# Order edges that hold each weight block's first-layer matmuls behind attention issued two blocks earlier

## The chip, the cores and the metric

The kernel runs on one core of one Trainium2 chip. The core has a matrix engine (TensorE, PE in the profile, with its weight loads shown apart as PEld), a vector engine (DVE), a scalar engine (ACT), GpSimd (POOL), and SyncE (SP), which here only starts transfers. Each engine works through its own list of instructions in order and waits on semaphores for the others. The metric is the device time of one execution in microseconds; less is better.

## The reference, cut to what matters

Everything is float32. Three stages follow each other, and each takes all of the one before:

```python
# 1. attention, batch 4, 8 heads, 512 local and 32 global positions, head size 64
s_g   = scale * q_g @ concat(k_g, k_l).T            # global queries see everything
out_g = softmax(s_g) @ concat(v_g, v_l)
s_ll  = where(abs(i - j) <= 32, scale * q_l @ k_l.T, -1e9)
a_l   = softmax(concat(scale * q_l @ k_g.T, s_ll))  # local ones a window and the globals
out_l = a_l @ concat(v_g, v_l)
x = concat(out_g, out_l) as (4, 576, 512)
# 2. first network, 512 -> 2048 -> 512, with a norm ahead and the input added back
xn = (x - mean) / sqrt(var + 1e-6) * g_ln
x  = x + relu(xn @ w_ch1) @ w_ch2
# 3. second network, 512 -> 1024 -> 512, gated by a 3-wide convolution over the sequence
h   = relu(x @ w_in)
out = (h * sigmoid(conv3(h))) @ w_out
```

## The kernel before, in words

**Attention** works on items. A local item is one batch, one tile of 128 queries and one pair of heads (64 of them, four to a tile); a global item is one batch and one pair of heads (16, spread among the local ones by `GAT`). An item takes these steps: its rows are loaded (`raw`), queries and keys are split into a rounded part and a remainder (`qs` on DVE and POOL, `kh` on ACT, `kl` on POOL), PE forms scores (`ps`, L273 and L274; a global item in two halves, L371 and L372), DVE takes them out of PSUM with mask and maximum (L277, L375), ACT does the exponentials (L286, L380), PE transposes (`pt` L299, `ptg` L393), ACT copies the result out (`ptsb`), and PE multiplies by the values (`po` L314 to L320, `pog` L402). Four items complete a tile; it is normed (`xn`, L443), transposed on PE (`ptx`, L455), and split by ACT and DVE (L106, L113) into `xe` or `xo`, which the first network reads. From item 23 on, all scores use one PSUM bank (`ps_a`, tag "s"), one unit of scores after the other. The first 16 items are a prologue of their own.

**The first network** works on chunks of tiles: one of three tiles, then seven of two (`CHUNKS`). Even chunks read `xe`, odd ones `xo`. For each chunk it goes through 16 weight blocks. A weight block is `hidden1` (12 first-layer matmuls of 256 columns, L669, into `ph`), a relu on ACT and its remainder on DVE (`hh` and `hl`, L678 and L679), and one block later `out1` (for each tile two matmuls on `hh` and one on `hl`, L692 to L697, into `yps`). I count blocks through: block 18 is the third block of chunk 1. In chunk 0 the third tile's `yps` occupies the bank "s".

**What sets the order.** The program is traced once and then put in order by a list scheduler: on each engine it issues, of what is ready by its own estimate of times, what has the best priority. Attention steps are traced from `tick` (L719), which is called some times in each block and hands `attend` (L518) a target that grows with the chunk (`PACE`), so that chunk c+1 is due a quarter chunk before chunk c ends. Within `attend` the steps get a priority 300 places ahead (`ahead(B_ATT)`). Nothing but readiness and priority ties the first network's matmuls to attention, other than the data: the first block of a chunk needs that chunk's `xe` or `xo`. In the last chunk (chunk 7) no attention is left, and the second network follows it.

Of the kernel before, what the change touches and what calls it, by code (L numbers as in the profile page):

```python
# [17 lines left out]
P = 128  # L18
# [4 lines left out]
NF, NF2, NDC = FF // P, F2 // P, DM // P  # L23
# [25 lines left out]
PACE = (0.25, 0), (0.88, 1), (1.8, 2), (2.75, 3)  # L49
CLEAD = 3.25  # L50
YLAG = 1
HB2 = 2

LATE = 7
# [7 lines left out]
def f32(ap):  # L62
    return ap.bitcast(F32)
# [3 lines left out]
def tile_kernel(ctx: ExitStack, tc: tile.TileContext, a_w, a_e, a_m, g_qk, g_v, w12, g_ln, w_io, conv_w, out):  # L67
    nc = tc.nc
    PE, DVE, ACT, POOL, SP = nc.tensor, nc.vector, nc.scalar, nc.gpsimd, nc.sync
# [14 lines left out]
    @contextmanager  # L84
    def ahead(n):
        p = tc.cur_priority
        tc.cur_priority = p - n
        yield
        tc.cur_priority = max(p, tc.cur_priority + n)

    def traced():
        return nc.cur_bb.bb.instructions
# [338 lines left out]
    chunks, at = [], 0  # L431
# [83 lines left out]
        add_step(i)  # L515
    pos = [0]

    def attend(upto):  # L518
        while pos[0] < min(upto, len(micro)):
            with ahead(B_ATT):  # L520
                micro[pos[0]]()
            pos[0] += 1

# [24 lines left out]
    def load_next(upto):  # L550
        while nload[0] < min(upto, NF if wpos[0] >= wdone[NF - 2] else NF - 1):
            load_w(nload[0], nload[0], w12[nload[0]])
            nload[0] += 1

    def convert(upto):
        while wpos[0] < min(upto, len(wq)):
            wq[wpos[0]]()
            wpos[0] += 1
# [18 lines left out]
    for i in range(first):  # L577
        slot, at = slots[i // PER], i % PER * RWH
# [7 lines left out]
    for k in range(1, len(slots)):  # L586
        n = min(PER, first - k * PER) * RWH
# [56 lines left out]
    def store_y(key, x):  # L644
        if key == "g":
            for b in range(B):
                SP.dma_start(yscr[b * S:b * S + SG, :], x[b * SG:(b + 1) * SG])
        else:
            b, t = key
            r = b * S + SG + t * P  # L650
            SP.dma_start(yscr[r:r + P, :], x)

    def first_network(items, tick, after_y, hpool, y_banks):

        hts, yps = {}, {}

        def edge(k, d):
            return not 0 <= k + d < len(items) or items[k + d][0] != items[k][0]

        def hidden1(k):  # L660
            ci, f = items[k]
            n = len(chunks[ci]) * P
            xth, xtl = xts[ci]
            convert(wdone[f])
            wh, wl = wt[f]
            ph = ps_h.tile([P, DM], F32, tag="h", name="ph")
            terms = [(w, x, d) for w, x in ((wh, xth), (wl, xth), (wh, xtl)) for d in range(NDC)]
            for m, (w, x, d) in enumerate(terms):
                PE.matmul(ph[:, :n], w[:, d * P:(d + 1) * P], x[:, d], start=m == 0, stop=m == 3 * NDC - 1)  # L669
                if m == 5:  # L670
                    tick(k)
            hh = hpool.tile([P, n], F32R, tag="hh", name="hh", bufs=HB2)
            if n > 2 * P:
                hl = early[:, k % 2 * n:][:, :n]
            else:
                hl = hpool.tile([P, n], F32R, tag="hl", name="hl", bufs=HB2)
            with ahead(B_RELU):
                ACT.activation(hh, ph[:, :n], AF.Relu)  # L678
                DVE.scalar_tensor_tensor(hl, ph[:, :n], 0.0, f32(hh), op0=ALU.max, op1=ALU.subtract)  # L679
            hts[k] = hh, hl  # L680
            tick(k)

        def out1(k):
            ci, f = items[k]
            hh, hl = hts.pop(k)
            wh, wl = wt[f]
            for i, key in enumerate(chunks[ci]):
                if edge(k, -1):
                    pool, tag = y_banks[i]
                    yps[i] = pool.tile([P, DM], F32, tag=tag, name="yps")  # L690
                tk = slice(i * P, (i + 1) * P)
                PE.matmul(yps[i], hh[:, tk], wh[:, DM:], start=edge(k, -1), stop=False)  # L692
                PE.matmul(yps[i], hh[:, tk], wl[:, DM:], start=False, stop=False)  # L693

            for i, key in enumerate(chunks[ci]):
                tk = slice(i * P, (i + 1) * P)
                PE.matmul(yps[i], hl[:, tk], wh[:, DM:], start=False, stop=edge(k, 1))  # L697
                if edge(k, 1):
                    x = xtiles[key].x
                    DVE.scalar_tensor_tensor(x, yps[i], xtiles[key].rstd, x, op0=ALU.mult, op1=ALU.add)  # L700
                    if f == NF - 1:
                        store_y(key, x)
                tick(k)
            after_y(k)

        for k in range(len(items) + YLAG):
            if k < len(items):
                hidden1(k)
            if k >= YLAG:
                out1(k - YLAG)  # L710

    last = len(chunks) - 1
    items = [(ci, f) for ci in range(last) for f in range(NF)]
    ends_at = [0] + [max(need[k] for k in chunks[ci + 1]) for ci in range(last)]
# [4 lines left out]
    def tick(k):  # L719
        ci = k // NF  # L720
        ticks[ci] += 1
        beats = 2 + CHUNKS[ci]
        at = ci + ticks[ci] / (beats * NF)
        for (t0, c), (t1, _) in zip(pace, pace[1:]):
            if t0 < at:
                attend(ends_at[c] + int((ends_at[c + 1] - ends_at[c]) * min((at - t0) / (t1 - t0), 1)))
        if ci == 0:
            load_next(LD3 + k)
            x = CLEAD + ticks[0] / beats
            done = [0] + [wdone[f] for f in range(NF)]  # L730
            f = int(x)
            convert(done[f] + int((done[f + 1] - done[f]) * (x - f)) if f < NF else done[NF])

    first_network(items, tick, lambda k: None, mpool,
                  [(ps_y, "y0"), (ps_y, "y1"), (ps_a, "s")])
    attend(len(micro))
    pa.close()

# [252 lines left out]
```

## Time and profile before

| | |
|---|---|
| runs, us | 765.64, 761.85, 766.15 (median 765.64) |
| profiled execution, us | 761.55 |
| its span, us | 759.7 |
| instructions in the span | 13043 |
| PE busy | 737.9 us, 97% |
| PEld / DVE / ACT / POOL busy | 87% / 60% / 48% / 31% |
| mean granted TensorE clock | 0.993 |

All other numbers are from the one profiled execution. Its own time is 1.85 us more than its span (761.55 against 759.7). Chunk 0 runs up to about 126 us, chunks 1 to 6 with attention beside them up to about 445 us in all, and after that PE has no attention left.

### The profile page before, as it was taken

The numbers are of one execution on the slowest core, as the hardware profiler recorded it, in microseconds if no ns is written. First come the engines' busy times: TensorE is split into PE (matmuls) and PEld (weight loads), VectorE is DVE, ScalarE is ACT, GpSimd is POOL, SyncE is SP. The second block draws the span as 40 slices with busy tenths as digits, with TensorE's granted clock in tenths as the row PEclk, the third lists the DMA queues.
The fourth block names the chain that finished last, engine by engine and source line by source line (L and its number), as shares of the span: only waits on it lengthen the run. The fifth ranks groups of instructions, "written<-read, shape, count | busy, mean of one in ns | idle before, by whom it ended". The sixth has DMA issues, their size and how long they took to land.

```text
span 759.7 us, 13043 instructions
## 1 busy us (share of the span) xinstructions
PE 737.9 (97%) x4841; PEld 664.7 (87%) x4841; DVE 457.7 (60%) x995; ACT 366.9 (48%) x871; POOL 235.4 (31%) x280
## 2 busy tenths in 40 slices
PE   9889999999999899989999999999999999999997
PEld 5778798998899799989998999998899998898996
DVE  4879974458564757576565743124966664555552
ACT  6768742456455455554544642114743353543431
POOL 1024330335343434454433530001324332332321
PEclk9999999999999899999999999999999999999999
DMA  9992231232433322243323310009520020200101
GB/s 371 425 415 82 76 111 38 70 94 84 125 88 99 110 79 85 84 130 100 87 75 102 84 35 28 0 19 354 206 83 1 1 86 16 81 4 1 57 1 69
DMA packets 30527, 77.08 MB, mean 101 GB/s; under 512 B 3712, under 2 KB 9856, under 8 KB 27392
## 3 DMA queue, kind: packets, MB, share of 16 engines
q1 hardware_dynamic: 29936, 75.42, 29.3%
q8 instruction: 38, 0.62, 0.3%
q10 hardware_dynamic: 528, 0.84, 0.3%
q14 instruction: 25, 0.20, 0.1%
HBM read 67.33 MB, written 8.91 MB: 100 GB/s over the span
## 4 chain that ended last, share of the span: by engine, by line
PE 55%; ACT 0%; DVE 0%; ACTq 0%; issue 0%
PE ph L669 12%; PE ph L829 4%; PE ph L831 4%; PE ph L830 4%; PE yps L697 4%; PE po L848 4%; PE yps L692 4%; PE yps L693 4%; PE po L849 4%; PE po L850 4%; PE pty L762 1%; PE pt L299 1%; PE po L320 1%; PE ps L274 1%; PE ps L273 1%; PE pog L402 0%
## 5 line engine op out<-in xcount | busy, mean ns | idle before, releaser
L669 PE MATMUL ph<-xe,w 128*128 128x256 f32 (+1 forms) x768 | 120.2, 300 | 4.7 <-ACT xe L106 3.5
L669 PEld LDWEIGHTS ph<-xe,w 128*128 128x128 f32 x768 | 110.7, 191 | 11.0 <-ACT xe L106 4.0
L669 PE MATMUL ph<-xo,w 128*128 128x256 f32 x768 | 111.1, 286 | 2.2 <-ACT xo L106 2.2
L113 POOL TENSOR_TENSOR kl<-raw,kh 128x384 fp32r<-128x384 f32 (+2 forms) x64 | 77.0, 1203 | 113.6 <-ACT kh L106 104.0
L692 PE MATMUL yps<-w,hh 128*128 128x512 f32 x272 | 110.1, 405 | 0.8 <-DVE x L330 0.4
L669 PEld LDWEIGHTS ph<-xo,w 128*128 128x128 f32 x768 | 103.1, 191 | 6.9 <-ACT xo L106 2.4
L693 PE MATMUL yps<-w,hh 128*128 128x512 f32 x272 | 107.9, 397 | 0.0
L678 ACT ACTIVATE hh<-ph 128x256 fp32r<-128x256 f32 (+1 forms) x128 | 50.2, 393 | 97.2 <-PE ph L669 89.7
L113 POOL TENSOR_TENSOR gl<-c,gh 128x544 fp32r<-128x544 f32 x32 | 44.2, 1380 | 135.6 <-ACT gh L106 135.6
L679 DVE SCALAR_TENSOR_TENSOR hl<-ph,hh 128x256 fp32r<-128x256 f32 x112 | 46.8, 419 | 64.6 <-ACT hh L678 63.6
L829 PE MATMUL ph<-yth,w 128*128 128x272 f32 x256 | 74.9, 293 | 0.0
L831 PE MATMUL ph<-yth,w 128*128 128x272 f32 x256 | 73.9, 289 | 0.0
L830 PE MATMUL ph<-ytl,w 128*128 128x272 f32 x256 | 73.8, 288 | 0.0
L697 PE MATMUL yps<-w,hl 128*128 128x512 f32 x224 | 72.7, 400 | 0.3 <-DVE hl L679 0.3
L286 ACT ACTIVATE sm<-sm,nm 128x192 f32<-128x192 f32 (+1 forms) x128 | 58.5, 459 | 16.5 <-DVE nm L277 16.1
L277 DVE CUSTOM_DVE_ANT_0 sm<-ps,mask 128x192 f32<-128x192 f32 (+1 forms) x128 | 42.3, 368 | 39.3 <-PE ps L274 28.7
L244 POOL TENSOR_TENSOR qs<-raw,qs 64x256 fp32r<-64x256 f32 x48 | 39.6, 824 | 68.6 <-ACT kh L106 22.7
L106 ACT ACTIVATE kh<-raw 128x384 fp32r<-128x384 f32 (+2 forms) x64 | 36.8, 577 | 49.7 <-issue 27.5
L692 PEld LDWEIGHTS yps<-w,hh 128*128 128x128 f32 x272 | 51.2, 188 | 7.7 <-ACT hh L678 1.0
L693 PEld LDWEIGHTS yps<-w,hh 128*128 128x128 f32 x272 | 51.3, 188 | 5.9
L834 DVE TENSOR_SCALAR c<-hs,cw 128x544 f32<-128x544 f32 x32 | 26.1, 816 | 49.9 <-ACT hs L832 48.0
L837 ACT ACTIVATE c<-c 128x544 f32<-128x544 f32 x32 | 21.1, 658 | 71.5 <-DVE c L836 68.9
(143 smaller groups left out, 1565.5 us busy)
## 6 DMA issues: line engine op xcount, KB each, us to landing
wraw<-w SPq DMA_DIRECT2D x16, 1024.0 KB, 17.1
raw<-a_m SPq DMA_DIRECT2D x24, 352.0 KB, 3.0
wraw<-w_io SPq DMA_DIRECT2D x8, 1024.0 KB, 6.6
raw<-a_e SPq DMA_DIRECT2D x25, 320.0 KB, 2.9
raw<-g_qk SPq DMA_DIRECT2D x16, 304.0 KB, 2.8
rawg<-g_v SPq DMA_DIRECT2D x16, 280.0 KB, 2.9
yr<-yscr SPq DMA_DIRECT2D x16, 256.0 KB, 3.4
yscr<-x SPq DMA_DIRECT2D x15, 256.0 KB, 2.0
```

The source lines that it names most:

```text
L113: e_lo.tensor_tensor(lo, src, f32(hi), op=ALU.subtract)
L277: DVE.tensor_tensor_reduce(out=s, in0=ps[j][:, :w], in1=mask[:, self.m0:self.m0 + w], scale=-0.125, scalar=BIG, op0=ALU.add, op1=ALU.min, ...
L286: ACT.activation(s, s, AF.Exp, bias=self.nm[:, j:j + 1], scale=-1.0, accum_out=xt.sums[:, h:h + 1])
L669: PE.matmul(ph[:, :n], w[:, d * P:(d + 1) * P], x[:, d], start=m == 0, stop=m == 3 * NDC - 1)
L678: ACT.activation(hh, ph[:, :n], AF.Relu)
L679: DVE.scalar_tensor_tensor(hl, ph[:, :n], 0.0, f32(hh), op0=ALU.max, op1=ALU.subtract)
L692: PE.matmul(yps[i], hh[:, tk], wh[:, DM:], start=edge(k, -1), stop=False)
L693: PE.matmul(yps[i], hh[:, tk], wl[:, DM:], start=False, stop=False)
L697: PE.matmul(yps[i], hl[:, tk], wh[:, DM:], start=False, stop=edge(k, 1))
L829: PE.matmul(ph, wh[:, w], yth[:, d, tk], start=d == 0, stop=False)
L830: PE.matmul(ph, wh[:, w], ytl[:, d, tk], start=False, stop=False)
L831: PE.matmul(ph, wl[:, w], yth[:, d, tk], start=False, stop=d == NDC - 1)
```

## The change

`attend` now notes for each of its PE instructions the block `k` in whose ticks it was traced. `hidden1(k)` wraps each of its twelve matmuls in `held(k)`: it looks up the last PE instruction of attention that was traced in block `k - 2` or earlier and adds an order edge behind it. The edge has no semaphore. It only tells the scheduler that on PE this matmul may not stand ahead of that instruction. No operation is added, removed or changed in size.

```diff
+HOLD = 2
-    def attend(upto):
+    issued = []
+
+    def attend(upto, k=0):
+        at = len(traced())
         while pos[0] < min(upto, len(micro)):
             with ahead(B_ATT):
                 micro[pos[0]]()
             pos[0] += 1
+        issued.extend((k, ins) for ins in traced()[at:] if ins.engine == mybir.EngineType.PE)
+
+    def held(k):
+
+        own = [ins for at, ins in issued if at <= k - HOLD]
+        return tc.issue_after(own[-1]) if own else nullcontext()
...
-                PE.matmul(ph[:, :n], w[:, d * P:(d + 1) * P], x[:, d], start=m == 0, stop=m == 3 * NDC - 1)
+                with held(k):
+                    PE.matmul(ph[:, :n], w[:, d * P:(d + 1) * P], x[:, d], start=m == 0, stop=m == 3 * NDC - 1)
...
-                attend(ends_at[c] + int((ends_at[c + 1] - ends_at[c]) * min((at - t0) / (t1 - t0), 1)))
+                attend(ends_at[c] + int((ends_at[c + 1] - ends_at[c]) * min((at - t0) / (t1 - t0), 1)), k)
```

Up to the first-layer matmuls of block 18 PE's list is the same as before. From there to the end of chunk 6 it differs; behind that it is the same again. Three places follow. Line numbers of the change are 11 higher for first-layer matmuls (L680) and `out1` (L703 to L708), and 1 higher for attention.

**Place 1**, PE's list at the start of chunk 1, behind the score unit `ps_1309`. `ph_1447`, `ph_1522`, `ph_1580` are the first-layer outputs of blocks 18, 19, 20; `ps_1367` and `ps_1395` are the halves of the next (global) item, `pt_1356` the transposes of the item of `ps_1309`. Before:

```order
L697 MATMUL yps_1442<-w_548,hl_1433 128x512
L669 MATMUL ph_1522<-xo_965,w_616 128x256 x8
L669 MATMUL ph_1522<-xo_966,w_616 128x256 x4
L692 MATMUL yps_1439<-w_566,hh_1494 128x512
L693 MATMUL yps_1439<-w_566,hh_1494 128x512
L692 MATMUL yps_1442<-w_566,hh_1494 128x512
L693 MATMUL yps_1442<-w_566,hh_1494 128x512
L697 MATMUL yps_1439<-w_566,hl_1495 128x512
L697 MATMUL yps_1442<-w_566,hl_1495 128x512
L669 MATMUL ph_1580<-xo_965,w_652 128x256 x5
L371 MATMUL ps_1367<-kh_1328,qs_1327 128x272
L372 MATMUL ps_1367<-kl_1329,qs_1327 128x272
```

With the change:

```order
L708 MATMUL yps_1442<-w_548,hl_1433 128x512
L372 MATMUL ps_1367<-kh_1328,qs_1327 128x272
L373 MATMUL ps_1367<-kl_1329,qs_1327 128x272
L300 MATMUL pt_1356<-ident_66,sm_94 112x128 x4
L372 MATMUL ps_1395<-kh_1328,qs_1327 128x272
L373 MATMUL ps_1395<-kl_1329,qs_1327 128x272
L680 MATMUL ph_1447<-xo_965,w_566 128x256 x8
L680 MATMUL ph_1447<-xo_966,w_566 128x256 x4
L321 MATMUL po_1190<-rawv_1146,ptsb_1361 128x64 x4
```

The block `ph_1447`, which stood ahead of `ps_1309` before, now stands behind three attention groups with no network matmul between them; `ph_1522` and `ph_1580`, which covered them before, have gone further back.

**Place 2**, PE's list five score units later, at `ps_1627`. Before, with block 25 (`ph_1828`) around it:

```order
L669 MATMUL ph_1828<-xo_965,w_867 128x256 x4
L371 MATMUL ps_1627<-kh_1571,qs_1570 128x272
L372 MATMUL ps_1627<-kl_1572,qs_1570 128x272
L669 MATMUL ph_1828<-xo_965,w_867 128x256 x4
L669 MATMUL ph_1828<-xo_966,w_867 128x256 x4
```

With the change, with block 19 (`ph_1522`) behind it:

```order
L274 MATMUL ps_1551<-kh_1499,qs_1498 128x224
L275 MATMUL ps_1551<-kl_1500,qs_1498 128x224
L372 MATMUL ps_1627<-kh_1571,qs_1570 128x272
L373 MATMUL ps_1627<-kl_1572,qs_1570 128x272
L403 MATMUL pog_1510<-v_1436,ptsb_1455 128x256 x5
L300 MATMUL pt_1539<-ident_66,sm_96 112x128 x4
L680 MATMUL ph_1522<-xo_965,w_616 128x256 x8
L680 MATMUL ph_1522<-xo_966,w_616 128x256 x4
```

The same attention stands six blocks earlier against the network, and here too several groups follow each other with no network matmul between them.

**Place 3**, PE's list at the end of chunk 1. `ptx_2070` are the transposes of the last tile of chunk 2, `ph_2207` is the first block of chunk 2. Before:

```order
L697 MATMUL yps_1442<-w_1214,hl_2180 128x512
L371 MATMUL ps_2092<-kh_2038,qs_2037 128x272
L372 MATMUL ps_2092<-kl_2039,qs_2037 128x272
L455 MATMUL ptx_2070<-ident_66,xn_2044 128x128 x4
L314 MATMUL po_2047<-rawv_1774,ptsb_2011 128x128
L315 MATMUL po_2047<-rawv_1774,ptsb_2011 128x64
L316 MATMUL po_2047<-rawv_1774,ptsb_2011 128x64
L299 MATMUL pt_2082<-ident_66,sm_94 128x128 x3
L669 MATMUL ph_2207<-xe_91,w_379 128x256 x8
```

With the change:

```order
L703 MATMUL yps_1442<-w_974,hh_1969 128x512
L315 MATMUL po_2047<-rawv_1774,ptsb_2011 128x128
L316 MATMUL po_2047<-rawv_1774,ptsb_2011 128x64
L317 MATMUL po_2047<-rawv_1774,ptsb_2011 128x64
L456 MATMUL ptx_2070<-ident_66,xn_2044 128x128 x4
L300 MATMUL pt_2082<-ident_66,sm_94 128x128 x3
L704 MATMUL yps_1442<-w_974,hh_1969 128x512
L708 MATMUL yps_1439<-w_974,hl_1970 128x512
L708 MATMUL yps_1442<-w_974,hl_1970 128x512
L680 MATMUL ph_2051<-xo_965,w_1087 128x256 x8
```

`ptx_2070` stood directly ahead of the block that reads its result; now it stands in the output matmuls of block 27, and blocks 29, 30 and 31 come between it and `ph_2207`.

## Rows read from the trace of the kernel before

**Rows 1.** The page: busy time, share of the span and instructions of each engine.
```profile
PE 737.9 (97%) x4841; PEld 664.7 (87%) x4841; DVE 457.7 (60%) x995; ACT 366.9 (48%) x871; POOL 235.4 (31%) x280
```
**Rows 2.** Stretches: length, PE, PEld, DVE, ACT, POOL busy, clock, DMA share, GB/s.
```profile
126.00:445.00 319.00, 311.09 (x2185) 288.37 (x2184) 198.05 (x548) 168.08 (x457) 130.91 (x134) 0.98 0.32 92
...
192.00:194.00 2.00, 1.45 (x7) 1.46 (x8) 1.08 (x4) 0.88 (x2) 0.00 (x0) 0.52 0.85 233
...
264.00:266.00 2.00, 2.00 (x12) 2.00 (x11) 0.00 (x0) 0.00 (x0) 0.00 (x0) 0.50 0.03 10
```
**Rows 3.** PE's waits, 126 to 445 us: total, times, longest, in us.
```profile
PE ph L669 <- ACT xe L106: 3.5, 2, 1.8
PE ph L669 <- ACT xo L106: 2.2, 1, 2.2
PE po L320 <- ACT ptsb L304: 0.8, 1, 0.8
PE ptx L455 <- DVE tmp L406: 0.8, 2, 0.4
...
PE pt L299 <- DVE tmp L406: 0.2, 1, 0.2
```
**Rows 4.** PE's timeline at three chunk boundaries: start, duration, [wait before, releaser].
```profile
192.55 3.47 PE L669 MATMUL ph<-xe,w 128*128 128x256 f32 x16 [1.75 <-ACT xe L106]
...
262.29 3.78 PE L669 MATMUL ph<-xo,w 128*128 128x256 f32 x16 [2.19 <-ACT xo L106]
265.87 1.63 PE L320 MATMUL po<-rawv,ptsb 112*128 112x64 f32 x8
...
333.33 2.16 PE L669 MATMUL ph<-xe,w 128*128 128x256 f32 x16 [1.76 <-ACT xe L106]
```
**Rows 5.** The timeline of DVE and ACT ahead of the first of these boundaries.
```profile
189.16 1.55 DVE L407 TENSOR_TENSOR ot<-tmp 64x128 f32<-64x128 f32 x1
...
190.75 0.71 ACT L416 ACTIVATE xg<-ot,recg 32x64 f32<-32x64 f32 x2 [1.67 <-DVE ot L407]
...
191.90 0.60 ACT L106 ACTIVATE xe<-ptx 128x512 fp32r<-128x512 f32 x1
```
**Rows 6.** PE's timeline at the start of chunk 1.
```profile
129.39 3.00 PE L669 MATMUL ph<-xo,w 128*128 128x256 f32 x24
132.23 0.39 PE L692 MATMUL yps<-w,hh 128*128 128x512 f32 x1
...
134.56 0.27 PE L273 MATMUL ps<-kh,qs 128*128 128x224 f32 x1
...
143.48 1.00 PE L320 MATMUL po<-rawv,ptsb 112*128 112x64 f32 x8
144.29 0.48 PE L692 MATMUL yps<-w,hh 128*128 128x512 f32 x1
...
160.31 0.60 PE L299 MATMUL pt<-ident,sm 128*112 128x128 f32 x4
```
**Rows 7.** The timelines of DVE, POOL and ACT in the same stretch.
```profile
135.20 0.39 DVE L277 CUSTOM_DVE_ANT_0 sm<-ps,mask 128x224 f32<-128x224 f32 x1 [0.76 <-PE ps L274]
...
135.83 1.26 DVE L243 CAST qs<-raw 128x256 fp32r<-128x256 f32 x1
...
139.77 0.43 DVE L375 CUSTOM_DVE_ANT_0 sm<-ps,tmpg 64x272 f32<-64x272 f32 x1 [1.77 <-ACT tmpg L374]
...
143.73 0.29 DVE L243 CAST qs<-raw 128x256 fp32r<-128x256 f32 x1 [2.21 <-PE ps L372]
...
144.52 0.69 DVE L330 TENSOR_TENSOR x<-po,rec 128x512 f32<-128x512 f32 x1 [0.16 <-PE po L320]
...
147.15 0.14 DVE L411 TENSOR_SCALAR recg<-sg 64x1 f32<-64x1 f32 x1
...
135.79 1.15 POOL L113 TENSOR_TENSOR kl<-raw,kh 128x448 fp32r<-128x448 f32 x1 [2.87 <-ACT kh L106]
...
136.49 0.19 ACT L286 ACTIVATION_READ_ACCUMULATOR sm<-sm,nm 128x1 f32 x1
```

## The prediction

> **What bounds the kernel now.** First the busy line [rows 1]: PE is busy 97% of the span, the next engine 60%. So work that is moved off PE's neighbours gives nothing; only what PE waits for, or runs slowly through, can be won. The change touches PE's list only from block 18 to the end of chunk 6, so the second view is that stretch by itself [rows 2]: from 126 to 445 us PE is busy 311.09 of 319.00 us. 7.9 us are idle, and the mean granted clock is 0.98. The third view says who ended these waits [rows 3]: 3.5 + 2.2 us for `xe` and `xo`, and 0.8 + 0.8 + 0.2 us for attention steps directly ahead of these, in all 7.5 us. Fourth, where: each wait for `xe` or `xo` is at a start of a chunk, at 192.55, 262.29 and 333.33 us [rows 4]. Fifth, why [rows 5]: at the first of them ACT writes the last part of `xe` at 191.90, because ahead of it in ACT's list L416 had waited for DVE's L407. Attention's last tile reaches PE directly ahead of the block that reads it (place 3), so such a chain has no cover.
>
> These waits also cost clock. The same 16 first-layer matmuls take 2.16 us at the third boundary, 3.47 at the first and 3.78 at the second [rows 4]; the granted clock behind those two was 0.52 and 0.50 [rows 2], the 1.2 GHz level, and ahead of both PE had waited. Against the third this is 1.31 + 1.62 us, and the value matmuls that follow the second take 1.63 against 1.00 us of the same group in a stretch at 2.4 GHz [rows 4, 6]: 0.63 more. Together **3.6 us**.
>
> **The change, part by part.**
>
> *Boundaries.* With the change `ptx_2070` is three whole blocks and more ahead of `ph_2207` (place 3). A block is some 4.2 us here (block 17 starts at 129.39, block 32 at 192.55 [rows 4, 6]); the wait it must cover was 1.75 us, with L407 and L416 (1.55 and 0.71 us) in it [rows 4, 5]. The order list shows the like at the other two boundaries. I take all of it as gone: **-7.5 us** of waits and **-3.6 us** of clock. Bounds: nothing, if the transposes should be late again by as much as they moved, and -11.1.
>
> *Catching up, first hold (place 1).* What pays for this is the start of chunk 1, where attention was behind and now PE's list waits for it. `ph_1447`'s twelve matmuls leave their place ahead of `ps_1309`: 24 such take 132.23 - 129.39 = 2.84 us, so twelve 1.42, one 0.118, and one of 512 columns I take as two of these [rows 6]. `ps_1309` therefore starts at 134.56 - 1.42 = 133.14, and four of its own matmuls and two of `yps` end at 134.06.
> - `ps_1367` needs the bank "s", which DVE frees with the second L277. Before, DVE went on to the next op at 135.83 for a start at 134.56, thus 1.27 later [rows 6, 7]: 134.41. PE waits 0.35 and works 0.24.
> - `pt_1356` needs both exponentials. They ended at 136.49 + 0.19 = 136.68, 2.12 behind `ps_1309` [rows 6, 7]: 135.26. PE waits 0.61 and works four matmuls, 0.47, to 135.73.
> - `ps_1395` needs the bank again, freed by L375. On DVE ahead of that stand the `qs` cast and two small ones of the reciprocal. The cast started 1.27 behind `ps_1309` and took 1.26 [rows 6, 7]: 135.67, two small ones like L411 at 0.14 make it 135.95, and L375 at 0.43 makes it 136.38. PE waits 0.65.
>
> Sum 1.6 us. Then `ph_1447` runs; its relu is used only after `po_1190` and `ps_1466`, so this is covered.
>
> *Second hold (place 2).* `ps_1627` needs the bank from `ps_1551`, and DVE has the norm of tile `x_1479` ahead of that L277. DVE's side, from the end of `po_1190`: 144.52 - 144.29 = 0.23 to L330, then L330 up to `xn`, 147.15 - 144.52 = 2.63, in which one L375 (0.43) no longer stands; but added are two pairs of L277 (0.63 each: 135.20 to 135.83) and three ops like L411 at 0.14 [rows 6, 7]. That is 0.23 + 2.63 - 0.43 + 1.26 + 0.42 = 4.11. PE's side, from the same point to the end of `ps_1551`: 13 matmuls of 0.118 and six of 0.236, 2.95. PE waits 1.2. What is queued behind it on PE (`pog_1510`, `pt_1539`, two whole blocks) waits with it, and nothing outside PE waits for these so soon. **+2.8 us** for both holds.
>
> Bounds. From below the two waits that no faster neighbour could remove, 0.35 + 0.61: +1.0. From above: before, attention took from 134.56 to 160.31, 25.75 us, from `ps_1309` to `pt_1616` [rows 6]; the work on PE now between these two is 72 short matmuls, 8 long ones and two value groups (0.81 each, 144.29 - 143.48 [rows 6]), some 12 us. Were attention no faster than it was, PE would wait 13.5. I stay near the lower end, since in the old stretch DVE and ACT mostly waited for PE (L277 and L375 have 0.76 and 1.77 us of it in front [rows 7]).
>
> In that sum the `qs` cast is 1.26 us, beside POOL's `kl` at 135.79; the same cast took 0.29 at 143.73, when POOL was not in the middle of one [rows 7]. With 0.29 the first hold is 0.5 shorter. The Trainium skill, SBUF — State Buffer (its terms, "shared port pair"), says that DVE and GpSimd lock one pair of ports for a whole instruction and that the loser blocks; the two rows agree. By that rule every cast of the catch-up would meet a POOL split, and one more cast at 1.26 would add up to 1.0.
>
> *Clock at the holds.* Two stretches of some 2.5 us in which PE waits half the time look like the boundaries, two of three of which lost clock [rows 4]. I count one loss of the smaller size, **+1.3**; bounds 0 and 2 x 2.25 (the second boundary's 1.62 + 0.63).
>
> *Other holds.* In chunks 1 to 6, 24 blocks now stand directly behind an attention group in the order list, 11 before. Before, such places cost nothing but at the boundaries: beyond the 7.5 us only 0.4 of the 7.9 us remain [rows 2, 3]. I take one wait of the size of the largest attention wait, 0.84, printed as 0.8 [rows 3]: **+0.8**; bounds 0 and 13 x 0.8 = 10.4.
>
> Edges cost no instruction and no semaphore, so nothing else is added. DMA loads and stores keep their order but for neighbours on SP's list that swap places; the DMA share is 0.32 in this stretch [rows 2].
>
> **Sum** against the profiled execution: 761.55 - 7.5 - 3.6 + 2.8 + 1.3 + 0.8 = 755.4. The profiled execution is 4.1 us below the median of the three runs (765.64). The trace doesn't say where the others lose this. I add 1.6 and forecast **757**, 1.1% below the median.
>
> **The rivals.**
>
> *A. The catch-up eats it.* The holds cost near the middle of their bounds, 8 us instead of 2.8, with two clock losses of 1.3: 755.4 + 5.2 + 1.3 = 762, or 763.5 with the 1.6. For it: place 1 and place 2 are chains over PE, DVE, ACT and POOL, and each hand-over costs something that I have only from offsets. Against it: no wait in the rows at these engines is longer than 2.2 us.
>
> *B. The gaps aren't lateness.* The gap repeats at three boundaries in the same size. If it came from a tile that finds no buffer, issuing attention earlier would only move it: 755.4 + 11.1 = 766.5, 768 with the 1.6. Against it: at the first boundary the last step ran as soon as ACT was through L416, behind L407 [rows 5]; that is order on an engine. The Trainium skill, Perfetto Trace Analysis (Identifying the Most-Contended Engine, under Optimization Strategy), reads consistent bubbles as a possible lack of SBUF or PSUM; here the rows name an instruction ahead in the list instead.
>
> *C. Slower: lockstep.* Each block may start only when attention of two blocks before is on PE, and attention is a chain through one bank. If the 24 blocks behind an attention group each wait the 0.84 us of [rows 3] and not one of them: 755.4 + 23 x 0.84 = 774.7, 776 with the 1.6, 1.4% above the median. It decides from 11.1 - 4.1 = 7.0 us on, 0.3 us per block. Against it: in the same stretch as many units of scores cost PE nothing before. For it: in the list attention now has two blocks of slack in place of six.
>
> **How the numbers follow.** Chances: forecast 0.60, A 0.20, B 0.09, C 0.11. The range goes from 751.5 (761.55 - 11.1 + 1.0, no clock loss) to 766, which takes in A and the spread of the runs; it leaves out C and most of B. A measurement of this kernel can tell about 1% from no change. Against 765.64 that is 758 and 773.3. Of the forecast's 0.60 some 0.44 lie below 758 and of A 0.04: faster 0.48. C gives slower 0.09 and the rest is the same, 0.43.
>
> **What would show it.** In the new profile, from 126 to 445 us: no wait of `ph` for `xe` or `xo` at a start of chunks 2 to 4, and clock 1.00 there; at 134 to 146 us some 3 us of PE waits, on L277, L375 or the exponentials, named at `ps`, `pt` or `pog`; chunk 6's end some 5 us earlier. A sum of PE waits over 8 us in that stretch would make A or C right; a wait at the boundaries that remains, B. The forecast is wrong if small waits stand at most blocks.

## The result, and the profile after

Median 755.25 us (755.10, 755.19, 755.31, 757.41) against 765.11 us of the kernel before (four runs): ratio 0.9885, 95% interval 0.985 to 0.992. The forecast was 757, 751.5 to 766. By the prediction's bound of 1% it is just "faster"; the interval reaches past that bound (0.992), so this isn't sure.

The profiled execution took 755.19 us (span 753.4, clock 0.997) against 761.55 before. The runs of the kernel before in this study lie between 761.7 and 766.5 us, and the mean clock goes with the time, from 0.993 in the fastest to 0.988 or 0.989 in the slowest; the profile that the prediction read is of the fastest kind.

The page's busy line and the stretches of the changed kernel, columns as in [rows 1, 2]:

```profile
PE 735.5 (98%) x4841; PEld 663.0 (88%) x4841; DVE 458.4 (61%) x995; ACT 366.1 (49%) x871; POOL 235.1 (31%) x280
```

```profile
126.00:445.00 319.00, 315.20 (x2243) 293.10 (x2241) 203.19 (x569) 172.27 (x474) 133.18 (x137) 0.99 0.32 93
146.00:148.00 2.00, 2.00 (x11) 2.00 (x11) 1.31 (x3) 0.88 (x2) 1.13 (x2) 0.50 0.19 28
192.00:194.00 2.00, 2.00 (x13) 1.73 (x12) 1.14 (x7) 1.68 (x5) 0.56 (x1) 1.00 0.69 192
264.00:266.00 2.00, 2.00 (x20) 2.00 (x19) 1.86 (x3) 0.49 (x2) 1.31 (x1) 1.00 0.58 173
```

From 126 to 445 us PE is idle for 3.80 us instead of 7.91. The two stretches that stood at 0.52 and 0.50 in [rows 2] are at 1.00; the 1.2 GHz level (0.50) now shows at 146 to 148 us. Read in steps of 2 us, the granted clock of this stretch is below full at 192 to 196 and 260 to 268 us before, and only at 144 to 150 us now. PE's same 4841 matmuls are busy for 2.4 us less in all, which goes with that clock. 4.1 + 2.4 makes 6.5; the span is 6.3 us shorter. PE's waits from 126 to 445 us, against [rows 3], in full:

```profile
PE ps L372 <- DVE nm L278: 3.1, 2, 2.6
PE ps L372 <- DVE nm L376: 0.6, 1, 0.6
```

None is at a boundary, and none lies behind 146 us. `xe` for chunk 2 was complete at 187.30 us, 11 us ahead of the first block that reads it (198.41). Chunk 7 starts 6.5 us earlier than before, at 500.67 against 507.19; some 5 were forecast. Attention's work on PE does not end at 445 us: its last transposes stand at 473 us before and at 467 with the change. In neither kernel does PE wait behind 445 us. PE's timeline at places 1 and 2:

```profile
134.96 0.36 PE L372 MATMUL ps<-kh,qs 128*128 128x272 f32 x1 [0.42 <-DVE nm L278]
135.16 0.29 PE L373 MATMUL ps<-kl,qs 128*128 128x272 f32 x1
135.29 0.78 PE L300 MATMUL pt<-ident,sm 128*112 128x128 f32 x4
136.66 0.40 PE L372 MATMUL ps<-kh,qs 128*128 128x272 f32 x1 [0.60 <-DVE nm L376]
...
144.95 0.36 PE L372 MATMUL ps<-kh,qs 128*128 128x272 f32 x1 [2.64 <-DVE nm L278]
...
145.28 1.34 PE L403 MATMUL pog<-v,ptsb 109*128 109x256 f32 x5
146.41 1.05 PE L300 MATMUL pt<-ident,sm 128*112 128x128 f32 x4
147.12 3.83 PE L680 MATMUL ph<-xo,w 128*128 128x256 f32 x24
150.79 1.00 PE L321 MATMUL po<-rawv,ptsb 112*128 112x64 f32 x8
```

The second hold is 2.64 us, not 1.2, and the 24 matmuls behind it take 3.67 us from start to start of the next group; the same number took 2.84 in [rows 6]. What DVE and POOL did meanwhile:

```profile
138.65 0.96 DVE L380 TENSOR_TENSOR nm<-nm 64x1 f32<-64x1 f32 x1
...
141.21 1.31 DVE L109 CAST qs<-raw 128x64 fp32r<-128x64 f32 x1
```

```profile
138.46 1.13 POOL L114 TENSOR_TENSOR kl<-raw,kh 128x448 fp32r<-128x448 f32 x1
...
141.11 1.35 POOL L114 TENSOR_TENSOR kl<-raw,kh 128x544 fp32r<-128x544 f32 x1 [1.52 <-ACT kh L107]
```

Both long DVE operations began while POOL was in a `kl` and ended with it (139.61 and 139.59, 142.52 and 142.46).

### The profile page after: what moved, and what is told of

The parts are those of the page before. It is cut to its first block, busy times and chain, and to the rows that moved or that the text cites. A ratio compares the mean times of both kernels' runs of the same rounds, so it can differ in the third digit from the quotient of the medians.

```text
span 753.4 us, 13048 instructions
## 1 busy us (share of the span) xinstructions
PE 735.5 (98%) x4841; PEld 663.0 (88%) x4841; DVE 458.4 (61%) x995; ACT 366.1 (49%) x871; POOL 235.1 (31%) x280
## 4 chain that ended last, share of the span: by engine, by line
PE 79%; DVE 1%; issue 0%; ACT 0%; ACTq 0%
PE ph L680 21%; PE yps L703 7%; PE yps L708 7%; PE yps L704 7%; PE ph L840 4%; PE ph L842 4%; PE ph L841 4%; PE po L859 4%; PE po L860 4%; PE po L861 4%; PE po L321 2%; PE pt L300 2%; PE pog L403 1%; PE pty L773 1%; PE ps L275 1%; PE ptg L394 1%
## 5 line engine op out<-in xcount | busy, mean ns | idle before, releaser
L680 PE MATMUL ph<-xe,w 128*128 128x256 f32 (+1 forms) x768 | 120.1, 298 | 1.2 <-DVE w L162 1.2
L680 PEld LDWEIGHTS ph<-xe,w 128*128 128x128 f32 x768 | 109.2, 188 | 6.5 <-DVE w L162 2.1
L703 PE MATMUL yps<-w,hh 128*128 128x512 f32 x272 | 110.0, 404 | 0.7 <-DVE x L331 0.4
L680 PE MATMUL ph<-xo,w 128*128 128x256 f32 x768 | 109.0, 285 | 0.0
L680 PEld LDWEIGHTS ph<-xo,w 128*128 128x128 f32 x768 | 102.0, 190 | 4.3
L708 PE MATMUL yps<-w,hl 128*128 128x512 f32 x224 | 73.2, 400 | 0.0
L278 DVE CUSTOM_DVE_ANT_0 sm<-ps,mask 128x192 f32<-128x192 f32 (+1 forms) x128 | 42.2, 368 | 34.3 <-PE ps L275 23.0
L703 PEld LDWEIGHTS yps<-w,hh 128*128 128x128 f32 x272 | 51.2, 188 | 7.4 <-ACT hh L689 1.0
```

Source lines behind the costliest of these rows:

```text
L278: DVE.tensor_tensor_reduce(out=s, in0=ps[j][:, :w], in1=mask[:, self.m0:self.m0 + w], scale=-0.125, scalar=BIG, op0=ALU.add, op1=ALU.min, ...
```

## The experiments

Times are medians; ratios stand against the kernel before, run on the same chip in turn. First theory, **cover**: a boundary waits when too little network work stands in PE's list between a chunk's last transposes and its first block, and catching up costs by how many blocks are pulled in at once. Rival, **spacing**: attention must be held in every block.

**Held in three blocks only.**

```diff
-        own = [ins for at, ins in issued if at <= k - HOLD]
+        own = [ins for at, ins in issued if at <= k - HOLD] if k <= 20 else []
```

> The hold acts in blocks 18 to 20 alone and on no later block. Attention is caught up once, at the start of chunk 1, and then drifts back in PE's list to four to seven blocks. Network work in the list between a chunk's last transposes (ptx) and the first block of that chunk, costed at 0.118 us a short and 0.236 us a long matmul from the rows of before: 9.2, 1.5, 1.4, 2.8, 5.4 us at blocks 32, 48, 64, 80, 96 (before: 0, 0, 0, 1.7, 5.7; with the change: 9.2, 6.6, 10.1, 11.8, 13.0). Cover theory (one catch-up is what pays; a boundary needs only some 2 us of cover): the catch-up waits of about 3.7 us stay; the wait at block 32 is gone, at 48 and 64 at most 0.3 to 0.8 us is left; sum of PE waits from 126 to 445 us 4 to 5 us, no second clock loss; profiled execution 755 to 757 us. Spacing theory (the gain needs every block to be held, so that PE keeps attention and network interleaved): waits of 1.8 to 2.2 us are back at two boundaries with the clock loss behind one, sum of PE waits about 8 us, time 760 us or more.

754.20 us, ratio 0.9858 (0.9835 to 0.9881). PE's waits from 126 to 445 us:

```profile
PE ps L372 <- DVE nm L278: 3.0, 2, 2.6
PE ps L372 <- DVE nm L376: 0.6, 1, 0.6
```

The same waits as with the change, and nothing at the boundaries. Three held blocks do all of it; spacing falls.

**Held late.**

```diff
-        own = [ins for at, ins in issued if at <= k - HOLD]
+        own = [ins for at, ins in issued if at <= k - HOLD] if k >= 32 else []
```

> The hold acts from block 32 on alone. Chunk 1 and the boundary at block 32 are those of the kernel before (no cover there), and the catching up of some five blocks happens at the start of chunk 2 instead. Cover theory: the wait for xe of 1.75 us and its clock loss of 1.3 us stay at block 32 (about 192 us), no wait at blocks 48 and 64; catching up costs PE waits of 2 to 4 us shortly behind 192 us and one clock loss of up to 1.7; time 756 to 759 us. Theory that the waits at 134 to 146 us belong to that place (chunk 0 has just freed the bank, the weights of the start are still being loaded) and not to the number of blocks pulled in at once: no waits of the catch-up anywhere, only 1.75 + 1.3 at block 32, time 752 to 753 us.

757.91 us, ratio 0.9906 (0.9883 to 0.9930). PE's timeline at the start of chunk 2:

```profile
193.08 0.39 PE L372 MATMUL ps<-kh,qs 128*128 128x272 f32 x1 [1.66 <-DVE nm L376]
...
196.94 1.40 PE L394 MATMUL ptg<-ident,sm 128*109 128x128 f32 x5 [0.68 <-ACT sm L381]
...
199.97 0.57 PE L372 MATMUL ps<-kh,qs 128*128 128x272 f32 x1 [0.83 <-DVE nm L278]
...
202.21 3.80 PE L680 MATMUL ph<-xe,w 128*128 128x256 f32 x24
```

The time fits cover; one detail doesn't: the wait for `xe` is gone too, since the caught-up attention stands ahead of the block. In its place are 3.2 us of catch-up waits and a slower clock. So catching up isn't bound to the place at 134 us.

**Held by and by.**

```diff
-        own = [ins for at, ins in issued if at <= k - HOLD]
+        hold = max(HOLD, 6 - max(k - 18, 0) // 3)
+        own = [ins for at, ins in issued if at <= k - hold]
```

> The hold reaches two blocks only by and by: six blocks at block 18, one less every three blocks, two from block 30 on. Cover at the boundaries 5.7, 6.6, 10.1, 11.8, 13.0 us at blocks 32, 48, 64, 80, 96 (estimate from the list as in the other runs). Cover theory, in which the cost of catching up depends on how many blocks are pulled in at once: no boundary wait; of the 3.7 us of PE waits at 134 to 146 us at most 1 us is left and of the 1.7 us of slower clock behind them at most 0.5; time about 751 us. Theory that catching up costs the same whenever it is done (each block of lag that is taken up is one stretch of attention without network beside it): the same 3.5 to 4 us of waits, spread from 134 to 185 us, time 754 to 756 us.

754.54 us, ratio 0.9856 (0.9831 to 0.9881). PE's waits, 126 to 445 us:

```profile
PE ps L372 <- DVE nm L278: 1.3, 1, 1.3
PE ps L372 <- POOL qs L114: 1.1, 1, 1.1
PE pog L403 <- DVE ptsb L398: 0.6, 1, 0.6
```

3.0 us of waits, now at 151 and 196 to 198 us. Cover theory's forecast of 751 was wrong: pulling in fewer blocks at once didn't make it cheap. The rival's time fits, its place (134 to 185 us) does not.

**Hold of four blocks.**

```diff
-HOLD = 2
+HOLD = 4
```

> The hold is four blocks instead of two, everywhere. Cover at the boundaries 3.1, 1.4, 4.5, 6.1, 9.2 us at blocks 32, 48, 64, 80, 96. Attention is behind by five to six blocks at block 18, so only one to two are pulled in. Cover theory: no wait at block 32 and 64, at most 0.8 us at block 48; waits at 134 to 146 us at most 1 us and no clock loss; time 751 to 752 us. Spacing theory (two blocks of distance matter by themselves): waits of about 2 us back at boundaries, time 757 us or more.

753.76 us, ratio 0.9853 (0.9828 to 0.9878). Its one wait in the whole stretch:

```profile
149.50 0.36 PE L372 MATMUL ps<-kh,qs 128*128 128x272 f32 x1 [2.61 <-DVE nm L278]
...
151.71 3.80 PE L680 MATMUL ph<-xo,w 128*128 128x256 f32 x24
```

No boundary wait, as cover had it, but its 751 to 752 us did not come: the second hold is there in full although fewer blocks are pulled in. Its price belongs to one spot, DVE's list ahead of that L278, which again had the cast at 1.30 and the 64x1 minimum at 0.96 us.

**Hold of five blocks.**

```diff
-HOLD = 2
+HOLD = 5
```

> The changed kernel with a hold of five blocks instead of two. Network work in PE's list between a chunk's last transposes and its first block: 1.7, 0.0, 1.7, 3.3, 5.4 us at blocks 32, 48, 64, 80, 96 (estimate from 0.118 us a short and 0.236 us a long matmul). Cover theory: a wait for xo of some 2 us comes back at block 48 (about 260 us) and there alone, with some 1.3 us of slower clock behind it; at 32 and 64 at most 0.5 us each. Hardly anything is caught up in chunk 1, so no wait of 2.6 us there; time 753 to 756 us. Theory that the hold itself and not the cover makes the difference (even interleaving): no wait at block 48, or waits at all three; times 751 or 760 us.

750.41 us, ratio 0.9820 (0.9798 to 0.9842). PE and ACT at block 48:

```profile
256.19 0.61 PE L456 MATMUL ptx<-ident,xn 128*128 128x128 f32 x4
256.63 0.60 PE L300 MATMUL pt<-ident,sm 128*112 128x128 f32 x4
257.38 0.39 PE L372 MATMUL ps<-kh,qs 128*128 128x272 f32 x1
257.61 0.29 PE L373 MATMUL ps<-kl,qs 128*128 128x272 f32 x1
257.74 2.06 PE L680 MATMUL ph<-xo,w 128*128 128x256 f32 x16
```

```profile
255.69 0.71 ACT L417 ACTIVATE xg<-ot,recg 32x64 f32<-32x64 f32 x2 [1.66 <-DVE ot L408]
...
256.42 0.40 ACT L375 ACTIVATE tmpg<-ps 64x272 f32<-64x272 f32 x1
...
256.84 0.60 ACT L107 ACTIVATE xo<-ptx 128x512 fp32r<-128x512 f32 x1
```

My forecast failed: no network work stands between `ptx` and `ph`, only attention's, and no wait came back. **Cover falls.** Here ACT was through L417 and L375 as `ptx` ended. This points to the chain on ACT and not to work on PE; the runs without a hold, below, test it.

**The cast on another engine.** A global item's first `qs` cast on ACT instead of DVE, with a hold of two, and then of four:

```diff
-            split(self.qs[:, :D], self.qs[:, D:P], self.raw[:, :D], DVE, POOL)
+            split(self.qs[:, :D], self.qs[:, D:P], self.raw[:, :D], ACT, POOL)
```

> The changed kernel with one operation on another engine: a global item's first part of the split queries (128x64, the cast that took 1.31 us on DVE at 141.21 us beside POOL's kl, 0.19 us in the kernel before) is written by ACT instead of DVE, for all 16 global items. Everything else is as with the change, hold of two blocks. Port theory (DVE stood still in that cast until POOL's kl was through, and this set the end of DVE's queue ahead of the L278 that PE waited for): DVE's queue is shorter by the cast, the wait of 2.64 us becomes 1.3 to 1.6 us, time 753 to 754 us. Order theory (the wait is the tile's norm and the two L278 that stand ahead on DVE, and a shorter DVE operation there is only followed by an equal wait, for ACT or for POOL): wait 2.3 to 2.7 us as before, time 755 us. Should the shorter wait also leave the TensorE clock at 2.4 GHz (the 24 matmuls behind it in 2.9 instead of 3.7 us), 1.7 us more are saved: 752 us.

> A hold of four blocks and the split queries of global items on ACT. With the hold of four alone one wait was left from 126 to 445 us, 2.61 us at 149.50 us, and behind it the 24 matmuls took 3.80 us at a granted clock of 0.50. On DVE ahead of that wait stood the 128x64 cast (1.30 us) and a 64x1 minimum (0.96 us), both ending with POOL's kl beside them. Port theory: the wait is 1.2 to 1.5 us; time 752.5 us, and 751 us if the clock stays up. Order theory: the wait stays 2.3 to 2.7 us and the time 753.8 us.

754.02 us, ratio 0.9867 (0.9845 to 0.9889), and 751.16, ratio 0.9833 (0.9807 to 0.9859). PE's timeline with a hold of two, then of four:

```profile
144.89 0.36 PE L372 MATMUL ps<-kh,qs 128*128 128x272 f32 x1 [1.47 <-POOL rstd L206]
...
146.25 3.09 PE L680 MATMUL ph<-xo,w 128*128 128x256 f32 x24
```

```profile
147.76 0.36 PE L372 MATMUL ps<-kh,qs 128*128 128x272 f32 x1 [1.45 <-POOL rstd L206]
...
148.09 0.85 PE L403 MATMUL pog<-v,ptsb 109*128 109x256 f32 x5
148.77 0.60 PE L300 MATMUL pt<-ident,sm 128*112 128x128 f32 x4
149.13 3.10 PE L680 MATMUL ph<-xo,w 128*128 128x256 f32 x24
152.06 1.00 PE L321 MATMUL po<-rawv,ptsb 112*128 112x64 f32 x8
```

2.64 became 1.47, 2.61 became 1.45: 1.2 us each, near the 1.1 by which the cast was longer than its 0.19 at 149.84 us in the kernel before. The port theory's waits came, and the clock stayed up behind both. These runs show that the cast's time on DVE counted; that POOL's `kl` set its length is read from the rows, where both end together. With a hold of two a new wait of 0.90 us, for POOL's `qs`, appeared at 260 us and took part of it back.

**The kernel before, profiled again.**

> The kernel before, once more, for a second profile. Its executions come in two groups, 761.7 to 762.2 us at a mean granted clock of 0.993 and 765.3 to 766.5 us at 0.988 to 0.989; the profile read for the prediction is of the first. If this one is of the second: clock theory: the same waits as in the first profile and some 4 us more of slower clock, part of it at the third chunk boundary (333 us), whose 16 first-layer matmuls then take 3.5 instead of 2.16 us. Wait theory: longer waits of PE somewhere, 3 to 4 us more idle time, and the lower mean clock only follows from them. If it is of the first group, nothing is told apart.

765.27 us, clock 0.989. PE's stretches, and its timeline at the third boundary:

```profile
126.00:445.00 319.00, 311.09 (x2159) 288.61 (x2159) 195.53 (x542) 165.50 (x450) 129.15 (x132) 0.97 0.31 91
...
268.00:270.00 2.00, 2.00 (x10) 2.00 (x11) 0.30 (x2) 0.79 (x2) 0.00 (x0) 0.50 0.20 57
...
337.00:339.00 2.00, 2.00 (x11) 2.00 (x11) 0.00 (x0) 0.00 (x0) 0.00 (x0) 0.50 0.77 264
```

```profile
335.69 3.01 PE L669 MATMUL ph<-xe,w 128*128 128x256 f32 x16 [1.75 <-ACT xe L106]
```

The same 7.91 us idle as in [rows 2], and PE busy 3.8 us longer (741.7). The third boundary, whose 16 matmuls took 2.16 us in [rows 4], is at 0.50 here, and behind the second the lower level lasts longer (0.50 at 268 to 270 us; 1.00 in the first profile). The clock theory holds: these 3.8 us are clock lost behind the boundary waits.

**What holds up ACT.** The kernel before, without any hold; first L416 on POOL, then also `tmpg` and `tmp`, which shared one buffer, in one each:

```diff
-                ACT.activation(xg[self.b * SG:(self.b + 1) * SG, h * D:(h + 1) * D], self.ot[o, j * D:(j + 1) * D],
-                               AF.Copy, scale=r[o])
+                POOL.tensor_scalar(xg[self.b * SG:(self.b + 1) * SG, h * D:(h + 1) * D], self.ot[o, j * D:(j + 1) * D],
+                                   r[o], None, op0=ALU.mult)
```

```diff
-            tmp = apool.tile([D, self.HALF], F32, tag="tmpg", name="tmpg")
+            tmp = apool.tile([D, self.HALF], F32, tag="tmph", name="tmpg")
```

> The kernel before, without the change, but with the two copies of a global item's result into xg (L416) on POOL instead of ACT. PE's list still has no network work between a chunk's last transposes and its first block at blocks 32, 48 and 64. Chain theory (the boundary waits come from L416, which stands on ACT ahead of the split that writes xe or xo and itself waits for DVE's L407, 1.45 to 1.56 us): ACT splits as soon as ptx is through, the three waits of 1.75, 2.19 and 1.76 us shrink to 0.5 us or less each, and with them goes the slower clock behind them; sum of PE waits from 126 to 445 us about 2 us instead of 7.5, time 751 to 756 us without any hold. Cover theory (what counts is network work between the transposes and the block, since copying and splitting ptx takes its time anyway): three waits of 1.2 to 2 us stay, time 760 to 764 us.

> The kernel before without the change, with L416's copies on POOL as in the run before, and the two temporary tiles tmp (read by L406 and L407) and tmpg (written by L374) in a buffer each instead of one for both. With L416 gone from ACT, ACT still stood idle for 1.74 us ahead of the boundary at block 32: L374 wrote tmpg at 191.59 us, just as DVE's L407, which works on tmp, had ended, and the split into xe (L106) stands behind L374. Buffer theory (L374 waits for the buffer that L407 still reads, and by this holds up the split): L374 runs at about 189.9 us, L106 as soon as ptx is through, the wait at block 32 falls from 1.08 to 0.2 us or less, and no boundary wait over 0.5 us is left; time 751 to 754 us without any hold, about the time of the changed kernel or less. Theory that ACT's L374 waits for something else (the scores in PSUM, PE): the wait of 1.08 us stays, time 756 us. Behind block 32 the scheduler's order differs in places from the run before, so the waits further on may lie elsewhere.

The first: 756.35 us, ratio 0.9904 (0.9886 to 0.9921). PE's boundary waits are 1.08, 1.94 and none; neither theory's number. ACT ahead of the first, and DVE:

```profile
191.59 0.39 ACT L374 ACTIVATE tmpg<-ps 64x272 f32<-64x272 f32 x1 [1.74 <-PE pt L299]
192.00 0.60 ACT L106 ACTIVATE xe<-ptx 128x512 fp32r<-128x512 f32 x1
```

```profile
189.94 1.55 DVE L407 TENSOR_TENSOR ot<-tmp 64x128 f32<-64x128 f32 x1
```

With L416 gone, L374 stood in the same gap. The profile names PE's `pt`, which has nothing to do with it; L407 had ended at 191.49. At the second boundary L374 stood behind L407 too, after 3.33 us without work on ACT. The second kernel: 750.80 us, ratio 0.9819 (0.9793 to 0.9845). Its ACT, and PE's waits from 126 to 445 us:

```profile
190.06 0.39 ACT L374 ACTIVATE tmpg<-ps 64x272 f32<-64x272 f32 x1
190.84 0.60 ACT L106 ACTIVATE xe<-ptx 128x512 fp32r<-128x512 f32 x1 [0.39 <-PE ptx L455]
```

```profile
PE ps L371 <- DVE nm L375: 1.0, 1, 1.0
PE ptx L455 <- DVE tmp L406: 0.4, 1, 0.4
```

The buffer theory holds: L374 ran 1.5 us earlier, the split right behind `ptx`, and no boundary waits. Two small edits win more than the hold, 750.80 against 755.25 us. The buffer alone, with L416 left on ACT, was not run.

Why L407 takes so long is in the rows of the kernel before, and was not followed up. Against its 1.55 us at 189.16 [rows 5]:

```profile
189.03 1.54 POOL L113 TENSOR_TENSOR v<-rawg,v 109x640 fp32r<-109x640 f32 x1
...
423.30 0.28 DVE L407 TENSOR_TENSOR ot<-tmp 64x128 f32<-64x128 f32 x1
```

Fifteen of the sixteen L407 took 1.10 to 1.56 us; each began while POOL was in a split (`v` or `kl`) and ended less than 0.2 us behind the end of one. The last one, with POOL idle, took 0.28. So the first link of the boundary chain is lengthened in the same way as the cast and the minimum of the second hold. Whether the waits would go if POOL's split ran at another time is not shown; no run moved it.

**Combinations.** Hold of five with the cast on ACT, and this with L416 on POOL (diffs as above).

> A hold of five blocks and the split queries of global items on ACT. With a hold of five alone 750.4 us were measured, with one wait of 1.15 us at 151 us, ended by L278 on DVE, and no slower clock behind it. Port theory: DVE's queue ahead of that L278 gets shorter only where POOL's kl runs beside the cast; at most the 1.15 us can be won: 749.3 to 750.4 us. If the wait is set by PE's short distance between the two score units and the tile's norm on POOL and DVE, nothing changes: 750.4 us.

> A hold of five blocks, the split queries of global items on ACT and L416's copies on POOL. If boundary waits and the clock behind them are all that there is to win between 126 and 445 us, nothing is left for the third step: same as with the first two, 749.3 to 750.4 us. If POOL's longer list delays the splits of keys (kl, qs) on it, waits for these appear at score units: 751 us or more.

750.29 us, ratio 0.9819 (0.9801 to 0.9837), and 750.50, ratio 0.9814 (0.9796 to 0.9832); one wait of 0.99 us is left in each. With the hold of five alone and the buffer kernel, four kernels end at 750.3 to 750.8, which this measurement can't tell apart; all are about 0.6% below the change.

## Why the prediction was right, point by point

The mechanism was right in the main: the boundary waits and their clock went, and holds at the start of chunk 1 were the price. That the sum came within 0.2 us was luck, as its errors cancelled.

- *Boundary waits, -7.5:* right. All are gone, with the 0.4 of small ones.
- *Why they were there:* half right. L407 and L416 ahead of L106 [rows 5] were the first half. The second, not seen, was the buffer that L407's input shares with the output of L374, which stood between L416 and L106 (at 191.48 us). Rival B's reason (a tile without a buffer) was thus true of ACT, while its consequence (the gap only moves) was not: with the change attention is early enough for ACT to have finished. The Trainium skill, Perfetto Trace Analysis (Optimization Strategy), reads consistent bubbles as a possible lack of SBUF or PSUM. I set the row's named instruction against it; for the second half, the runs with and without the shared buffer (756.35 and 750.80 us) agree with the page.
- *Clock at the boundaries, -3.6:* right against that profile. PE is busy 2.4 us less although the holds cost 1.5 of clock, which makes 3.9.
- *First hold, 1.6:* measured 0.42 + 0.60. The terms 0.35 and 0.65 were near; the 0.61 for `pt_1356` didn't come: `pt` started right behind L373, and only its weight loads stood 0.2 us for an exponential inside the group.
- *Second hold, 1.2:* the term that failed, 2.64. The working took each small operation that DVE gets ahead of that L278 at 0.14 us; beside POOL's `kl` the 64x1 minimum took 0.96 and the 128x64 cast 1.31. The cast stood in the stretch that I summed; the minimum ran just ahead of it, and L331 began 0.62 us behind `po_1190`, where the sum had 0.23. The runs with the cast elsewhere give 1.2 of the 1.4 missing. The Trainium skill, SBUF — State Buffer (its terms, "shared port pair"), has DVE and GpSimd lock each other out for a whole instruction; by the 1.0 that I priced for it and set aside, the hold would have been 2.2. The rows agree with the page.
- *Clock at the holds, +1.3:* right in kind. Against the 1.45 us case, whose clock stayed up, `pog` took 1.13 for 0.68, `pt` 0.71 for 0.36 and the 24 matmuls 3.67 for 2.93, start to start: 1.5 us.
- *Other holds, +0.8, and rival C:* nothing. No PE wait lies behind 146 us, so the price per held block was zero here.
- *Rival A:* holds and their clock cost 3.7 + 1.5 of the 11.5 won. A had 8 + 2.6. What stood against A, that no wait at these engines was longer than 2.2 us, was misread: [rows 7] has 2.87 us of POOL idle for ACT's `kh`.
- *The sum, 755.4:* by measured terms 761.55 - 7.9 - 3.6 + 3.7 + 1.5 = 755.3; measured 755.19. The second hold's 1.4 too little was cancelled by the first hold's 0.6 and the other holds' 0.8 too much: luck, not accuracy.
- *The 1.6 for the spread:* nothing of it came. The second profile of before loses 3.8 us more of clock behind the very waits that the change removes. The changed kernel's median (755.25) is that of its profile (755.19), and the gain against the median is 9.9 where the profiles show 6.4. Without the 1.6 the forecast would have been 755.4 instead of 757.

## What to carry to other kernels

When a split or copy that PE waits for is late, list what stands ahead of it on its own engine and ask of each instruction which buffer it writes and who still reads that: here giving two tiles a buffer each, with one copy moved to another engine, won more than the reordering. Where an order constraint only has to cure a lag, try weaker ones too: five blocks beat two and four here, since the price lay in one crowded spot and not in the number of edges (constant holds of three and six were not run). In a sum for a stretch where DVE and POOL will work side by side, price each small DVE operation at the length that the trace shows beside a POOL operation.

## What the hardware showed unexpectedly

- The granted clock behind a wait of PE: after 1.15, 1.45 and 1.47 us it stayed at 2.4 GHz, after 2.19, 2.61 and 2.64 us it fell to 1.2 GHz. After 1.75 us at the first boundary it fell in both profiles of the kernel before; after 1.75 to 1.76 us at the third it stayed in one and fell in the other. With a longer stay at the lower level behind the second boundary this makes 3.8 us between two executions of one kernel.
- A DVE operation on 64x1 elements took 0.96 us beside POOL's `kl`, and 0.13 at 146.09 us in the kernel before, when POOL was in none; the 128x64 cast took 1.31 us, and 0.19 at 149.84 us in the kernel before, begun while POOL was idle. L407 took 1.10 to 1.56 us beside a split and 0.28 without.
- The releaser that a profile names can be a bystander: `tmpg <- pt L299`, 1.74 us, was a wait for a buffer that DVE was still reading.
